# Channel-mix units of 448 tokens that run across batch ends, weights decoded in place of their doubles, shared scratch slots, exponentials in place

## The chip, the cores and the metric

The kernel runs on one core of a Trainium2 chip. The core has five engines with a program each: TensorE (PE, with its weight loads listed apart as PEld), VectorE (DVE), ScalarE (ACT), GpSimd (POOL) and SyncE (SP), which here issues every DMA. They meet at semaphores only. The metric is the device time of one execution in microseconds, lower is better. Three runs of the kernel before took 711.98, 712.05 and 712.50 us, with a median of 712.05.

## The reference

Eight batches of 576 tokens go through windowed attention (8 heads of 64, each query sees its own and the 63 keys before it) and then through a channel mix with two hidden products and a gate:

```python
def _attn_ref(q, k, v):
    scores = scale * np.matmul(q, k.transpose(0, 1, 3, 2))
    mask = (rel >= 0) & (rel < 64)
    scores = np.where(mask, scores, -1e9)
    scores = scores - np.max(scores, axis=-1, keepdims=True)
    attn = np.exp(scores)
    attn = attn / (np.sum(attn, axis=-1, keepdims=True) + 1e-09)
    return np.matmul(attn, v)

def _moe_ref(x, mu_k, mu_r, w_k, w_v, w_r):
    x_prev = ...                       # x one token earlier, zero at a batch's start
    xk = mu_k * x + (1.0 - mu_k) * x_prev
    xr = mu_r * x + (1.0 - mu_r) * x_prev
    k = np.maximum(xk @ w_k, 0.0)      # 512 -> 1024
    v = k * k @ w_v                    # 1024 -> 512
    r = 1.0 / (1.0 + np.exp(-(xr @ w_r)))
    return r * v
```

The weights come as float64, everything else as float32.

## The kernel before

**Attention.** Heads are taken in pairs, which fill the 128 partitions, and a pair's nine blocks of 64 queries in three groups of three. For a group, `scores` makes three score matmuls into PSUM tile `s` (line 149), subtracts mask and finds the minimum on DVE into tile `sm` (152), takes the exponential on ACT into tile `pr` (155), and divides on POOL by the sums (158 to 161). `flip` transposes the three blocks on PE into tile `t` (168) and copies them out (170). `mix_v` takes two groups at once: 12 matmuls of 64 by 64 into tile `x` (182), copied into `xT` (187), which holds a whole batch, channels on partitions; there are two such buffers. Each of these three is a stage; a batch has 42 stages, the later ones of a group behind the next group's first.

**Channel mix.** A unit is half a batch, 288 tokens, so there are 16 units. `time_mix` makes `xr` and `xk` from `xT` chunk by chunk (221 to 226), each split into two float32r parts. The weights are split into two parts too, so each product takes three matmuls per 128 by 128 block of weights: x0 w0, x1 w0, x0 w1 (line 235). Per unit that is 48 matmuls for the gate `r`, 96 for `k` and 96 for `v`: 240, each with 128x128 weights and 288 columns, in 20 steps of 12. ACT, POOL and DVE bring each result out (247 to 253 for the gate, 262 to 266 for the squared hidden values `ks`, 275 for the output), and SP writes it (276). Results go through four PSUM tiles `m`.

**Weights.** 20 chunks of 128 by 512 doubles are loaded into three rotating tiles `wst`, taken apart on DVE by five instructions each (107, 108, 109, 111, 113), and written by ACT and POOL into the tiles `wr_s`, `wk_s`, `wv_s` (116, 117). Twelve chunks are handed out during the first batch's attention, the other eight in the first eight steps of the first unit.

**Order.** The program runs the first batch's attention, mixes the first unit, and then goes through the 320 steps of the units. Each step hands out one attention stage, every sixteenth step two; from step 11 of a unit on, the next unit's mixing goes along. This is only the order in which work is handed to a scheduler, which puts each engine's instructions in an order of its own by dependences, free buffers and an estimated clock. The engines then execute these lists strictly in order.

Of the kernel before, what the change touches and what calls it, by code (L numbers as in the profile page):

```python
# [9 lines left out]
F32 = mybir.dt.float32  # L10
# [32 lines left out]
def attn_rwkv_kernel(ctx, tc, qT, kT, v2, mu_k, mu_r, w_k, w_v, w_r, out):  # L43
# [12 lines left out]
    # queries of a pair by block, the heads' apart: zero where a head's rows meet the  # L56
    # other head's columns
# [24 lines left out]
    # the first group's weights: its first block has none for the other keys  # L82
# [7 lines left out]
    wk_s = const.tile([P, 2, NC, DF], F32R, name="wk_s")  # L90
    wr_s = const.tile([P, 2, NC, DM], F32R, name="wr_s")
    wv_s = const.tile([P, 2, NF, DM], F32R, name="wv_s")

    # A weight comes as a double: its low word and its high word. The float's bits are
    # sign and top exponent bit of the high word, its next 27 bits and 3 bits of the low
    # word; a magnitude outside float32's normal range is brought to its ends first.
    def weights():
        for dst, src in ((wr_s, w_r), (wk_s, w_k), (wv_s, w_v)):
            for c in range(0, dst.shape[3], WC):
                for i in range(dst.shape[2]):  # L100
                    st = tmp.tile([P, WC, 2], U32, name="wst", bufs=WB)
                    nc.sync.dma_start(st.rearrange("p c t -> p (c t)"),
                                      src[i * P:(i + 1) * P, c:c + WC].bitcast(U32))
                    lo, hi = st[:, :, 0], st[:, :, 1]
                    t = tmp.tile([P, WC], U32, name="wt")
                    tf = t.bitcast(F32)
                    nc.vector.tensor_scalar(t, hi, 0x7FFFFFFF, None, op0=ALU.bitwise_and)  # L107
                    nc.vector.tensor_scalar(tf, tf, HI_MIN, HI_MAX, op0=ALU.max, op1=ALU.min)  # L108
                    nc.vector.tensor_scalar(t, t, 3, 0x3FFFFFF8,  # L109
# [5 lines left out]
                    w0, w1 = dst[:, 0, i, c:c + WC], dst[:, 1, i, c:c + WC]  # L115
                    nc.scalar.copy(w0, tf)  # L116
                    nc.gpsimd.tensor_sub(w1, tf, w0.bitcast(F32))  # L117
                    yield

# [1 line left out]
    loaded = {}  # L121
# [245 lines left out]
```

## Time and profile before

| | |
|---|---|
| median of three runs | 712.05 us |
| profiled execution, first to last instruction (span) | 711.3 us |
| around it, to the median | 0.75 us |
| matmul records on PE | 5856, of them 3840 of the channel mix (line 235) |
| busy: PE, DVE, ACT, POOL | 682.2, 415.5, 413.9, 364.9 us |

The page's second part cuts the span into 40 slices of 17.8 us; each digit is the busy share in tenths, 9 being 90% and more. PEclk is the granted TensorE clock, in tenths of full speed.

```profile
PE   6878878999999999999999999999999999999998
DVE  3999999955545455465535455463645556463421
ACT  4768775663626383748566575756756475644351
PEclk9999898999999999999999999999999999999999
```

The first eight slices differ from the rest: there DVE is full and PE is not, afterwards PE is full and no other engine is. The columns of a group row in the views below are: line, engine, operation, output from inputs, shapes, count, then busy us and mean ns of one, then the idle time ahead of them and what ended it. A timeline row has start, length, engine, line, operation and count. Matmuls overlap, so a matmul's own mean time (some 300 ns) is not the distance between two of them; that is read from the starts of rows.

### The profile page before, as it was taken

The page shows a single profiled execution, that of the slowest core. Times are in us where ns is not written, and L with a number is a line of the kernel's source. Part 1 is how long each engine was busy: PE and PEld are TensorE (multiplying, and loading weights), DVE is VectorE, ACT ScalarE, POOL GpSimd, SP SyncE. Part 2 cuts the span into 40 slices and gives each one's busy share as a digit, 9 for nine tenths or more (in the row PEclk, how much of TensorE's full clock was granted, in tenths as well). Part 3 has the DMA queues.
Part 4 walks back from the last instruction along what each step waited for, and adds up shares of the span by engine and source line. Part 5 has one row for each costly group of instructions (what it writes and reads, how often), then busy time and mean ns, then how long its engine had stood idle before and what let it go on. Part 6 is the DMA issues. An engine that isn't in the chain of part 4 may idle for free.

```text
span 711.3 us, 15989 instructions
## 1 busy us (share of the span) xinstructions
PE 682.2 (96%) x5856; PEld 657.9 (92%) x5856; DVE 415.5 (58%) x1326; ACT 413.9 (58%) x1397; POOL 364.9 (51%) x580
## 2 busy tenths in 40 slices
PE   6878878999999999999999999999999999999998
PEld 5766777799999999999999999999999999999998
DVE  3999999955545455465535455463645556463421
ACT  4768775663626383748566575756756475644351
POOL 4788898754335272554626355453624546252420
PEclk9999898999999999999999999999999999999999
DMA  8885666620000001221222222211323221000000
GB/s 208 237 234 152 189 178 176 166 73 26 10 34 2 34 31 64 65 89 45 85 63 72 68 64 88 73 55 44 95 66 94 67 64 48 18 1 35 26 9 34
DMA packets 59742, 56.61 MB, mean 80 GB/s; under 512 B 40592, under 2 KB 49040, under 8 KB 59664
## 3 DMA queue, kind: packets, MB, share of 16 engines
q1 hardware_dynamic: 59664, 55.59, 26.7%
q8 instruction: 46, 0.75, 0.5%
q14 instruction: 32, 0.26, 0.1%
HBM read 46.14 MB, written 9.44 MB: 78 GB/s over the span
## 4 chain that ended last, share of the span: by engine, by line
PE 80%; DVE 15%; POOL 1%; issue 1%; DMA 1%; SPq 1%; ACT 0%
PE m L235 68%; PE s L149 6%; PE x L182 4%; PE t L168 3%; DVE sm L152 2%; DVE wt L111 2%; DVE wt L107 2%; DVE wt L113 2%; DVE xm L224 1%; DVE wt L109 1%; DVE wt L108 1%; DVE rs L158 1%; POOL pr L161 1%; DMA qbd<-qT 1%; DVE d L221 1%
## 5 line engine op out<-in xcount | busy, mean ns | idle before, releaser
L235 PE MATMUL m<-ks,wv_s 128*128 128x288 f32 x1536 | 226.1, 301 | 1.0 <-ACT wv_s L116 0.9
L235 PE MATMUL m<-xk,wk_s 128*128 128x288 f32 x1536 | 221.2, 299 | 2.0 <-POOL wk_s L117 2.0
L161 POOL TENSOR_SCALAR pr<-pr,rs 128x128 f32<-128x128 f32 (+1 forms) x288 | 129.7, 467 | 173.0 <-DVE rs L159 62.4
L235 PEld LDWEIGHTS m<-ks,wv_s 128*128 128x128 f32 x1536 | 208.7, 190 | 2.5 <-ACT wv_s L116 1.3
L235 PEld LDWEIGHTS m<-xk,wk_s 128*128 128x128 f32 x1536 | 207.0, 189 | 3.6 <-POOL wk_s L117 2.2
L155 ACT ACTIVATE pr<-sm,nmax 128x128 f32<-128x128 f32 (+1 forms) x288 | 111.6, 391 | 68.0 <-DVE nmax L152 67.9
L263 POOL TENSOR_TENSOR kf<-kf 128x288 f32<-128x288 f32 x128 | 93.2, 733 | 81.1 <-ACT kf L262 80.1
L266 DVE TENSOR_TENSOR ks<-kf,ks 128x288 fp32r<-128x288 f32 x128 | 72.6, 571 | 71.5 <-ACT ks L265 71.3
L235 PE MATMUL m<-xr,wr_s 128*128 128x288 f32 x768 | 113.1, 299 | 1.0 <-POOL xr L226 1.0
L235 PEld LDWEIGHTS m<-xr,wr_s 128*128 128x128 f32 x768 | 103.5, 188 | 2.4 <-POOL xr L226 1.9
L149 PE MATMUL s<-k,qbd 128*128 128x128 f32 (+1 forms) x576 | 88.4, 294 | 15.7 <-DVE nmax L152 9.0
L149 PEld LDWEIGHTS s<-k,qbd 128*128 128x128 f32 x576 | 79.0, 205 | 19.0 <-DVE nmax L152 11.2
L226 POOL TENSOR_TENSOR xr<-xm,xr 128x288 fp32r<-128x288 f32 x64 | 56.4, 891 | 71.2 <-ACT xr L225 68.4
L152 DVE CUSTOM_DVE_ANT_0 sm<-s,mask 128x128 f32<-128x128 f32 (+1 forms) x288 | 66.7, 276 | 36.1 <-PE s L149 36.0
L262 ACT ACTIVATE kf<-m 128x288 f32<-128x288 f32 x128 | 52.2, 409 | 36.8 <-PE m L235 29.5
L224 DVE SCALAR_TENSOR_TENSOR xm<-d,muk,xT 128x288 f32<-128x288 f32 x64 | 55.2, 862 | 26.7 <-POOL xr L226 26.6
L265 ACT CAST ks<-kf 128x288 fp32r<-128x288 f32 x128 | 55.1, 431 | 24.9 <-POOL kf L263 24.5
L253 DVE SCALAR_TENSOR_TENSOR r<-th,e 128x288 f32<-128x288 f32 x64 | 34.2, 535 | 50.4 <-ACT th L251 50.1
L247 ACT ACTIVATE e<-m 128x288 f32<-128x288 f32 x64 | 26.2, 410 | 60.9 <-PE m L235 60.7
L168 PE MATMUL t<-ident,pr 128*128 128x128 f32 x288 | 55.4, 284 | 6.2 <-POOL pr L161 3.4
L275 DVE SCALAR_TENSOR_TENSOR r<-m,r 128x288 f32<-128x288 f32 x64 | 28.3, 451 | 56.4 <-PE m L235 56.4
L226 POOL TENSOR_TENSOR xk<-xm,xk 128x288 fp32r<-128x288 f32 x64 | 58.5, 933 | 5.2 <-ACT xk L225 5.2
(44 smaller groups left out, 652.7 us busy)
## 6 DMA issues: line engine op xcount, KB each, us to landing
v<-v SPq DMA_DIRECT2D x32, 512.0 KB, 3.6
outT<-r SPq DMA_DIRECT2D x64, 144.0 KB, 1.7
k<-kT SPq DMA_DIRECT2D x31, 288.0 KB, 3.1
qbd<-qT SPq DMA_DIRECT2D x62, 144.0 KB, 3.6
wst<-w_k SPq DMA_DIRECT2D x8, 512.0 KB, 4.1
wst<-w_v SPq DMA_DIRECT2D x8, 512.0 KB, 3.6
wst<-w_r SPq DMA_DIRECT2D x4, 512.0 KB, 7.6
k<-kT SPq DMA_DIRECT2D x1, 192.0 KB, 2.4
```

The source lines that it names most:

```text
L149: nc.tensor.matmul(ps[:, j, :nk], q[:, i].rearrange("p h r -> p (h r)"), k[:, k0:k0 + nk], start=True, stop=True)
L152: nc.vector.tensor_tensor_reduce(sm[:, j, :nk], ps[:, j, :nk], mask if nk == P else mask0, scale=-SCALE, scalar=FAR, op0=ALU.add, op1=ALU.min,
L155: nc.scalar.activation(pr[:, j, :nk], sm[:, j, :nk], AF.Exp, bias=nmax[:, j:j + 1], scale=-1.0, accum_out=sums[:, j:j + 1])
L161: nc.gpsimd.tensor_scalar(pr[:, j, :nk], pr[:, j, :nk], rs[:, j:j + 1], 1.0, op0=ALU.mult, op1=ALU.mult)
L168: nc.tensor.transpose(ps[:, j, :], pr[:, j, :], ident)
L224: nc.vector.scalar_tensor_tensor(xm, d, mu[:, c:c + 1], xp, op0=ALU.mult, op1=ALU.add)
L226: nc.gpsimd.tensor_sub(xs[:, 1, c], xm, xs[:, 0, c].bitcast(F32))
L235: nc.tensor.matmul(ps, w[:, a, c, col * P:(col + 1) * P], x(c, e), start=(i == 0), stop=(i == last))
L262: nc.scalar.activation(kf, ps, AF.Relu)
L263: nc.gpsimd.tensor_mul(kf, kf, kf)
L265: nc.scalar.copy(ks[:, 0], kf)
L266: nc.vector.tensor_sub(ks[:, 1], kf, ks[:, 0].bitcast(F32))
```

## The change

The two first units keep 288 tokens, then come nine of 448: 2 x 288 + 9 x 448 = 4608 = 8 x 576. Six of the nine hold tokens of two batches; for those `time_mix` makes two pieces of each of its DVE instructions, and the output takes two transfers. There are 11 units and 220 steps. Attention stages are handed out so that a unit's last batch is complete when its mixing begins, in equal shares between these points: 34 stages in the first 31 steps, then 42 in each 20 steps, none where a unit needs no new batch (steps 92 to 111), again 42 in each 20 up to step 171.

The decoded weights take, chunk by chunk, slots of the same 20 that the doubles are loaded into (tag `w`). The scratch tiles `d`, `xm`, `e`, `th`, `kf` and `wt`, which had buffers of their own, share six slots (tag `tmp`). The exponential is made in place: `sm` is gone, DVE writes the scores into `pr`, which has three buffers where it had two.

```diff
-TH = S // 2          # tokens of a MoE unit
+UNITS = (288, 288) + (448,) * 9
+TU = max(UNITS)
+USTEPS = 20
+TB = 6
...
-    wk_s = const.tile([P, 2, NC, DF], F32R, name="wk_s")
...
-                    st = tmp.tile([P, WC, 2], U32, name="wst", bufs=WB)
...
-                    t = tmp.tile([P, WC], U32, name="wt")
...
+                st = const.tile([P, WC, 2], U32, name="w", tag="w", bufs=len(chunks))
...
+            tf = tmp.tile([P, WC], F32, name="wt", tag="tmp", bufs=TB)
...
+            ws[i, c] = const.tile([P, 2, WC], F32R, name="ws", tag="w", bufs=len(chunks))
...
-        sm = at.tile([P, G, P], F32, name="sm", bufs=3)
-        pr = pr0 if g == 0 else at.tile([P, G, P], F32, name="pr")
+        pr = pr0 if g == 0 else at.tile([P, G, P], F32, name="pr", bufs=3)
...
-            nc.vector.tensor_tensor_reduce(sm[:, j, :nk], ps[:, j, :nk], mask if nk == P else mask0,
+            nc.vector.tensor_tensor_reduce(pr[:, j, :nk], ps[:, j, :nk], mask if nk == P else mask0,
...
-            nc.scalar.activation(pr[:, j, :nk], sm[:, j, :nk], AF.Exp, bias=nmax[:, j:j + 1], scale=-1.0,
+            nc.scalar.activation(pr[:, j, :nk], pr[:, j, :nk], AF.Exp, bias=nmax[:, j:j + 1], scale=-1.0,
...
+    def parts(u):
+        t, end = sum(UNITS[:u]), sum(UNITS[:u + 1])
+        found = []
+        while t < end:
+            n = min(end, (t // S + 1) * S) - t
+            found.append((t // S, t % S, n))
+            t += n
+        return found
...
+            d = tmp.tile([P, TU], F32, name="d", tag="tmp", bufs=TB)
+            for b, t0, nt in parts(u):
+                xT = xTs[b]
+                x, xp = xT[:, c, 1 + t0:1 + t0 + nt], xT[:, c, t0:t0 + nt]
+                nc.vector.tensor_sub(d[:, o:o + nt], x, xp)
...
+                xm = tmp.tile([P, TU], F32, name="xm", tag="tmp", bufs=TB)
+                for o0, o1, xp in pieces:
+                    nc.vector.scalar_tensor_tensor(xm[:, o0:o1], d[:, o0:o1], mu[:, c:c + 1], xp,
+                                                   op0=ALU.mult, op1=ALU.add)
...
-            run(ats, 1)
-            if done % 16 == 0:
-                run(ats, 1)
...
+    goals = [(0, staged)] + [((u - 1) * USTEPS + MIX_AT, STAGES * (parts(u)[-1][0] + 1))
+                             for u in range(2, len(UNITS))]
+            for (s0, a0), (s1, a1) in zip(goals, goals[1:]):
+                if s0 < done <= s1:
+                    goal = a0 + -(-(a1 - a0) * (done - s0) // (s1 - s0))
+                    run(ats, goal - staged)
+                    staged = goal
```

In the new kernel line 269 is the matmul of line 235, 161 the score matmul, 180 the transpose and 194 the matmul into `x`.

How the scheduler's order moves is shown at three places of PE's list. The first is where the channel mix begins. Before, the first gate product `m` of unit 0 stands behind eight groups of scores `s`:

```order
L149 MATMUL s<-k,qbd_82 128x64
L149 MATMUL s<-k,qbd_82 128x128 x5
L182 MATMUL x<-pt,v 64x64 x6
L168 MATMUL t<-ident,pr 128x128 x3
L182 MATMUL x<-pt,v 64x64 x6
L235 MATMUL m<-xr,wr_s 128x288 x4
L149 MATMUL s<-k,qbd_82 128x128 x3
L235 MATMUL m<-xr,wr_s 128x288 x8
```

Now, at the same product:

```order
L180 MATMUL t<-ident,pr_114 128x128 x2
L194 MATMUL x<-pt,v 64x64 x6
L180 MATMUL t<-ident,pr_114 128x128
L269 MATMUL m<-xr,ws 128x288 x4
L180 MATMUL t<-ident,pr 128x128 x3
L194 MATMUL x<-pt,v 64x64 x3
L269 MATMUL m<-xr,ws 128x288 x8
```

It has moved behind 23 groups: DVE's list has the first mixing of unit 0 behind ten decoded chunks, where it stood behind one. The second place is the end of unit 0, its products into the output (`m<-ks`). Before, they stand among attention, here their first 24 of 96:

```order
L235 MATMUL m<-ks,wv_s 128x288 x4
L149 MATMUL s<-k,qbd_83 128x64
L149 MATMUL s<-k,qbd_83 128x128 x2
L168 MATMUL t<-ident,pr_114 128x128 x3
L235 MATMUL m<-ks,wv_s 128x288 x6
L149 MATMUL s<-k,qbd_83 128x128 x3
L182 MATMUL x<-pt,v 64x64 x6
L235 MATMUL m<-ks,wv_s 128x288 x8
L168 MATMUL t<-ident,pr 128x128 x3
L182 MATMUL x<-pt,v 64x64 x6
L235 MATMUL m<-ks,wv_s 128x288 x6
```

Now they are one run, with nothing of attention among them:

```order
L269 MATMUL m<-xk,ws 128x288 x24
L161 MATMUL s<-k,qbd_83 128x128 x3
L269 MATMUL m<-ks,ws 128x288 x96
L269 MATMUL m<-xr,ws 128x288 x20
L194 MATMUL x<-pt,v 64x64 x3
L269 MATMUL m<-xr,ws 128x288 x28
```

The third place stands for the rest of PE's list, a gate product in the middle. Before, the 12 matmuls into `x` of two groups are one run:

```order
L235 MATMUL m<-xr,wr_s 128x288 x12
L168 MATMUL t<-ident,pr 128x128 x3
L235 MATMUL m<-xr,wr_s 128x288 x12
L182 MATMUL x<-pt,v 64x64 x12
L235 MATMUL m<-xr,wr_s 128x288 x12
L149 MATMUL s<-k,qbd_83 128x128 x3
L235 MATMUL m<-xr,wr_s 128x288 x12
```

Now they are cut in two, with other work between:

```order
L180 MATMUL t<-ident,pr_114 128x128 x3
L269 MATMUL m<-xr,ws 128x448 x5
L194 MATMUL x<-pt,v 64x64 x6
L269 MATMUL m<-xr,ws 128x448 x8
L180 MATMUL t<-ident,pr 128x128 x3
L194 MATMUL x<-pt,v 64x64 x6
L269 MATMUL m<-xr,ws 128x448 x10
L161 MATMUL s<-k,qbd_82 128x128 x3
```

Over all of PE's list, the 48 pairs of groups make 70 runs of `x` before and 103 now. Behind the last mixed stretch of the start (before: the gate products of unit 1; now: the run of 96 above) these lists still hold 51, 58 and 59 groups of `s`, `t` and `x` in 33 runs of `x` before, and 61, 66 and 70 in 77 runs now.

More of the change, by code (lines that the diff above doesn't have):

```diff
@@ L234, in product @@
             for a, e in ((0, 0), (0, 1), (1, 0)):
-                nc.tensor.matmul(ps, w[:, a, c, col * P:(col + 1) * P], x(c, e),
+                nc.tensor.matmul(ps, weight(w, a, c, col), x(c, e),
                                  start=(i == 0), stop=(i == last))
@@ L275, in v_units @@
             nc.vector.scalar_tensor_tensor(o, ps, 0.5, o, op0=ALU.mult, op1=ALU.mult)
-            nc.sync.dma_start(out[b, m * P:(m + 1) * P, half * TH:(half + 1) * TH], o)
+            c0 = 0
+            for b, t0, nt in parts(u):
+                nc.sync.dma_start(out[b, m * P:(m + 1) * P, t0:t0 + nt], o[:, c0:c0 + nt])
+                c0 += nt
             yield
     def new_mixed():
-        return [act.tile([P, 2, NC, TH], F32R, name=nm) for nm in ("xr", "xk")]
+        return [act.tile([P, 2, NC, TU], F32R, name=nm) for nm in ("xr", "xk")]
     def run(g, n=None):
@@ L309, in attn_rwkv_kernel @@
     mixed = new_mixed()
-    run(time_mix(xTs[0], 0, *mixed))
+    run(time_mix(0, *mixed))
     run(ats, LEAD)
+    staged = STAGES + LEAD
+    goals = [(0, staged)] + [((u - 1) * USTEPS + MIX_AT, STAGES * (parts(u)[-1][0] + 1))
+                             for u in range(2, len(UNITS))]
     done = 0
-    for u in range(B * 2):
-        b, half = divmod(u, 2)
+    for u in range(len(UNITS)):
         xr, xk = mixed
@@ L320, in steps @@
         def steps():
-            yield from r_units(xr, gate)
-            yield from k_units(xk, k2)
-            yield from v_units(b, half, k2, gate)
+            yield from r_units(xr, gate, UNITS[u])
+            yield from k_units(xk, k2, UNITS[u])
+            yield from v_units(u, k2, gate)
         for n, _ in enumerate(steps()):
```

100 lines of the change are left out of this document (55 added, 45 removed).

## The prediction

> **What bounds the kernel now.** I read the busy time by stretch first, then the chain of waits. The columns of the stretches are PE, PEld, DVE, ACT and POOL busy with instruction counts, then granted clock, DMA share and GB/s.
>
> ```profile
> 20.00:146.00 126.00, 107.31 (x1001) 92.68 (x1002) 121.52 (x438) 90.75 (x342) 108.23 (x152) 0.93 0.63 184
> 146.00:246.00 100.00, 100.00 (x758) 100.00 (x757) 52.78 (x94) 47.16 (x132) 39.88 (x51) 1.00 0.09 29
> 246.00:628.00 382.00, 382.00 (x3419) 374.43 (x3419) 202.12 (x689) 236.49 (x808) 184.21 (x317) 1.00 0.22 63
> ```
>
> From 146 us on PE is never idle while no other engine passes 62% (ACT, 236.49 of 382). From 20 to 146 us DVE is busy 121.52 of 126 us and PE waits for it. The chain of waits says the same: in the first stretch it runs through DVE lines (decoding 107 to 113, scores 152), in the second through matmuls alone.
>
> ```profile
> by line: DVE sm L152 13.5%; DVE wt L111 12.8%; DVE wt L107 10.3%; DVE wt L113 10.0%; DVE xm L224 8.0%; DVE wt L109 7.5%; DVE wt L108 6.8%; DVE rs L158 4.8%; POOL pr L161 4.4%; issue 4.4%; DVE d L221 4.2%; DVE ks L266 2.9%; DVE rs L159 2.2%;
> ...
> 145.94 98.47 PE m L235 x744
> ```
>
> So there are two questions: when does PE become full, and how much work is left on PE from there. Before, the first answer is 145.9 us and the second 711.3 - 145.9 = 565.4 us.
>
> **The product matmuls.** The 744 of that row take 98.47 us, so a 288-column matmul costs 132.35 ns. What part of it grows with columns? A stretch in which the throttle gave half the clock helps:
>
> ```profile
> 107.80:114.50 6.70, 5.89 (x33) 5.20 (x32) 6.60 (x21) 2.75 (x11) 6.22 (x8) 0.50 0.27 81
> ...
> 112.90 1.64 PE L235 MATMUL m<-ks,wv_s 128*128 128x288 f32 x6
> ...
> 113.62 0.92 PE L235 MATMUL m<-ks,wv_s 128*128 128x288 f32 x3
> ```
>
> Three matmuls later the same run starts 0.72 us later: 240 ns each at half clock, 0.833 ns per column. At full clock the streaming should be half, 120 ns, so 12.35 ns of the 132.35 are something else. For 448 columns the streaming is 448 x 0.4167 = 186.7 ns. That is the lower end. The upper end is that all 132.35 ns grow with columns: 205.9 ns. I take the excess as a cost per matmul, 199.1 ns, between the two; the rows don't settle it.
>
> It isn't the weight load. A load has the same form for scores as for products, and six loads with six matmuls pass in 0.68 us (below), 113 ns each, so the load would be ready before 132 ns are over:
>
> ```profile
> L235 PEld LDWEIGHTS m<-xk,wk_s 128*128 128x128 f32 x1536 | 207.0, 189 | 3.6 <-POOL wk_s L117 2.2
> ...
> L149 PEld LDWEIGHTS s<-k,qbd 128*128 128x128 f32 x576 | 79.0, 205 | 19.0 <-DVE nmax L152 11.2
> ```
>
> The Trainium skill, page "TensorE: Matmul & The Clock Gate", section "Back-to-back issue gap", puts the gap of two matmuls at N/1.2 ns on the slow clock and at N/2.4 + 2.5 ns on the fast one. The first is what the trace has (240 ns), the second would be 122.5 ns and differs from the measured 132.35. By it 448 columns would take 189.2 ns and the 2160 wide matmuls 408.7 us, an estimate from that page.
>
> Behind the point at which PE is full, the old kernel has 3600 product matmuls: 476.5 us. The new one has 336 of 288 columns (44.5 us) and 9 x 240 = 2160 of 448 (430.1 us at 199.1 ns). The term is **-1.9 us**. It is small because 96 products of unit 0 that were done during the start are now behind it (12.7 us); in like for like, 3360 narrow ones at 444.7 us become 430.1.
>
> **The attention left for the full stretch.** Costs on PE from starts of rows, products at 0.1324 us taken out:
>
> ```profile
> 402.14 1.84 PE L235 MATMUL m<-xr,wr_s 128*128 128x288 f32 x12
> 403.82 0.49 PE L168 MATMUL t<-ident,pr 128*128 128x128 f32 x3
> 404.06 1.84 PE L235 MATMUL m<-xr,wr_s 128*128 128x288 f32 x12
> 405.83 0.92 PE L182 MATMUL x<-pt,v 128*64 128x64 f32 x24
> 406.68 1.85 PE L235 MATMUL m<-xr,wr_s 128*128 128x288 f32 x12
> 408.37 0.83 PE L149 MATMUL s<-k,qbd 128*128 128x128 f32 x6
> 408.95 1.84 PE L235 MATMUL m<-xr,wr_s 128*128 128x288 f32 x12
> ```
>
> From 402.14 to 404.06 are 1.92 us, less 12 x 0.1324 = 1.59: a group's transposes cost 0.33 us. In the same way its scores cost 408.95 - 406.68 - 1.59 = 0.68, and two groups' `x` (24 records for 12 matmuls) 406.68 - 404.06 - 1.59 = 1.03. Where `x` was cut:
>
> ```profile
> 348.06 0.54 PE L235 MATMUL m<-ks,wv_s 128*128 128x288 f32 x2
> 348.53 0.57 PE L182 MATMUL x<-pt,v 128*64 128x64 f32 x12
> 349.03 0.40 PE L235 MATMUL m<-ks,wv_s 128*128 128x288 f32 x1
> 349.36 0.45 PE L182 MATMUL x<-pt,v 128*64 128x64 f32 x6
> 349.73 0.66 PE L235 MATMUL m<-ks,wv_s 128*128 128x288 f32 x3
> ```
>
> 12 records cost 0.97 - 0.26 = 0.71 us, 6 cost 0.70 - 0.13 = 0.57. From 12 to 24 records is 0.32 us, 0.027 per record; the rest, **0.38 us, is paid for every run of `x`** however short (0.41 by the 6). So the cutting seen in the order costs: 77 runs behind the start instead of 33, 44 x 0.38 = 16.7 us. Ten more groups of scores are 6.8 us, eight more of transposes 2.6 us, eleven groups of `x` 11 x 12 x 0.027 = 3.6 us. Together **+29.7 us**.
>
> What is left on PE: 565.4 - 1.9 + 29.7 = 593.2 us.
>
> **When PE is full.** Before, the last chunk leaves DVE at 140.27 + 0.74 = 141.0 us:
>
> ```profile
> 140.27 0.74 DVE L113 SCALAR_TENSOR_TENSOR wt<-wst,wt 128x512 uint32<-128x512 uint32 x1
> ```
>
> The decoding is unchanged, 5 x 20 instructions. What else stands ahead of that instruction in DVE's list is less: 33 groups of scores instead of 41 and as many pairs of `rs` instead of 38, 4 `d` instead of 11, 8 `xm` instead of 19, 5 `ks` instead of 8. DVE's groups from 20 to 146 us:
>
> ```profile
> L152 DVE CUSTOM_DVE_ANT_0 sm<-s,mask 128x128 f32<-128x128 f32 (+1 forms) x111 | 25.7, 270 | 0.0
> L111 DVE SCALAR_TENSOR_TENSOR wt<-wst,wt 128x512 uint32<-128x512 uint32 x20 | 19.3, 963 | 0.2
> L113 DVE SCALAR_TENSOR_TENSOR wt<-wst,wt 128x512 uint32<-128x512 uint32 x20 | 17.0, 850 | 0.1
> L107 DVE TENSOR_SCALAR wt<-wst 128x512 uint32<-128x512 uint32 x19 | 14.1, 741 | 2.1 <-POOL wk_s L117 1.5 <-POOL wr_s L117 0.6
> L109 DVE TENSOR_SCALAR wt<-wt 128x512 uint32<-128x512 uint32 x20 | 11.9, 596 | 0.1
> L108 DVE TENSOR_SCALAR wt<-wt 128x512 f32<-128x512 f32 x19 | 10.3, 540 | 0.1
> L158 DVE TENSOR_SCALAR rs<-sums 128x3 f32<-128x3 f32 x35 | 8.9, 254 | 1.8 <-ACT pr L155 1.8
> L152 DVE DVE_READ_ACCUMULATOR2_ANT nmax<- 128x1 f32 x111 | 8.6, 77 | 0.0
> L221 DVE TENSOR_TENSOR d<-xT 128x288 f32<-128x288 f32 x11 | 6.8, 623 | 0.0
> L224 DVE SCALAR_TENSOR_TENSOR xm<-d,mur,xT 128x288 f32<-128x288 f32 x10 | 5.9, 594 | 0.0
> L224 DVE SCALAR_TENSOR_TENSOR xm<-d,muk,xT 128x288 f32<-128x288 f32 x9 | 5.9, 659 | 0.0
> L159 DVE RECIPROCAL rs<-rs 128x3 f32<-128x3 f32 x36 | 5.9, 163 | 0.0
> L266 DVE TENSOR_TENSOR ks<-kf,ks 128x288 fp32r<-128x288 f32 x8 | 4.6, 572 | 0.0
> L253 DVE SCALAR_TENSOR_TENSOR r<-th,e 128x288 f32<-128x288 f32 x4 | 2.3, 590 | 0.0
> L275 DVE SCALAR_TENSOR_TENSOR r<-m,r 128x288 f32<-128x288 f32 x4 | 1.5, 437 | 0.0
> ```
>
> Less are 24 x (0.270 + 0.077) + 5 x (0.254 + 0.163) + 11 x 0.625 + 7 x 0.623 + 3 x 0.572 = 23.4 us by these means. The rows overlap: they add up to 148.7 us in 121.5 us of busy time, a factor of 0.82, so 19.1 us go, and the last chunk is done at 121.9 us. Behind it, ahead of the last `ks` of unit 0, stand 3 `ks`, 2 `d` and 3 `xm`: 4.8 us by the means, 4.0 with the factor. PE can run the first 12 output products (1.6 us) ahead of the last `ks`. PE is full from 121.9 + 4.0 - 1.6 = **124.3 us**. Bounds: 121 us if all of the 23.4 us count (with the 4.8 behind), 134 if the mixing taken out was only filling and the pace is set by attention's chain.
>
> This is earlier by 21.6 us, but 27.8 us of work more are left then: the start covers less of PE's work than it did, because the mixing of unit 0 comes so late that its output products find no place beside DVE.
>
> **What costs nothing.** The wider work of ACT, DVE and POOL lies beside PE. By the busy row of 246 to 628 us ACT fills 62%, and one wide instruction takes the place of 1.56 narrow ones. Attention comes twice as densely in some units and not at all in others, but PE's steps are longer by half too; that in-order queues meet in time is what I rely on, and 1 us of stall is 1 us of time, as PE has no slack. The doubled pieces at batch ends are 12 short DVE instructions in each of six units, and by the same row DVE is free for 47% of the time. The exponential in place removes a buffer, no work; where DVE then waits for a transpose in the start, that is the upper bound above. The shared room and slots remove no instruction.
>
> **Sum.** 124.3 + 593.2 = 717.5 us of span. The median lies 0.75 us above the profiled span; that makes **718.2 us**, 0.9% slower.
>
> **Rivals.** (a) Nothing but streaming grows: the 12.35 ns are hidden by the longer matmul. At 186.7 ns the 2160 cost 26.8 us less: **691 us**, faster. It decides from 196.3 ns per wide matmul downwards, 6.1 us over 2160 below my 199.1. For it: at half clock the excess is nil, so it can vanish. Against: scores pass at 113 ns per load, so the excess is not a load that a longer matmul would cover. Chance 0.15. The formula of the Trainium skill, page "TensorE: Matmul & The Clock Gate", section "Back-to-back issue gap", is of this kind; by its 189.2 ns the time would be 697 us, an estimate from that page. (b) The excess grows with columns: 205.9 ns, +14.7 us, **733 us**. For it: the same vanishing at half clock fits a limit on reading columns. Chance 0.15. (c) The start is shorter: without the mixing among them the attention groups pass faster, and PE is full at 112 us: **706 us**, faster. Against: DVE was idle for only 4.5 of those 126 us, so its list would have to shrink, not its waits. Chance 0.12. (d) The start is longer, as DVE, writing into `pr`, waits for transposes, or dense attention makes stalls: 10 us more, **728 us**. Chance 0.10. My forecast keeps 0.48, with a range of its own of 706 to 728 us: the start's bounds, and below them half the price of the cuts, as only two rows show it.
>
> **How the numbers follow.** A measurement of this kernel can tell some 0.2%, 1.4 us, from no change. Faster: nearly all of (a), most of (c), and a seventh of the forecast, whose range crosses 710.6: 0.32. Within 0.2%: 0.09. Slower: 0.59. The range leaves out (a) and the far half of (b): 700 to 735 us.
>
> **What would show it.** The distance of the wide matmuls in a pure run: 199 ns; 187 is (a), 206 is (b). The start of the run of 96 output products of unit 0: 122 to 125 us; below 115 is (c), above 132 is (d). Runs of `x` of 12 records at some 0.7 us each in the mixed stretches; were they 0.5, 9 us of my sum are gone. PE should still be busy 100% behind the start; idle slices there would be a stall that I haven't counted.

## The result, and the profile after

The changed kernel takes **735.86 us** (median of four runs, 731.59 to 738.68), the kernel before on the same chip 712.01 (711.44 to 712.50). The ratio is **1.033, with an interval of 1.029 to 1.037**: 3.3% slower. The forecast was 718.2 us, 0.9% slower, with a range of 700 to 735; the side is right, the size is not, and the time lies just above the range. The profiled execution has a span of 735.6 us, 18.1 above the 717.5 of the forecast's sum. The explanation goes by this span.

The busy tenths of the page, in slices of 18.4 us:

```profile
PE   6777988699999999899999999999999999999997
DVE  3989788647257337633732923483357336428221
ACT  4667774264754765475344557556745763453530
PEclk9878899899999999999999999999999999999999
```

Of the second to the eighth slice, in which DVE was full (9), only two are full now. PE's digits are lower in three of the first eight slices and higher in two, and the clock row has a 7 and four 8s where it had two 8s. The stretches say it in numbers, in the columns used before:

```profile
20.00:146.00 126.00, 100.12 (x797) 87.04 (x798) 106.23 (x354) 75.55 (x271) 97.23 (x131) 0.86 0.53 155
146.00:246.00 100.00, 99.24 (x716) 91.11 (x714) 52.19 (x149) 55.95 (x162) 45.35 (x62) 1.00 0.19 59
246.00:628.00 382.00, 378.19 (x2557) 337.86 (x2554) 190.09 (x651) 219.68 (x650) 164.54 (x253) 1.00 0.21 61
```

From 20 to 146 us DVE is busy 106.23 us instead of 121.52, so the start has waits that it did not have, and the granted clock is 0.86 instead of 0.93. And behind 146 us PE is no longer full: it misses 0.76 and 3.81 us, where it missed none. The view of PE's waits from 200 to 700 us names what it waits for (us in total, times, longest), 4.2 of 4.5 us in these two rows:

```profile
PE t L180 <- ACT pt L182: 3.2, 2, 1.9
PE x L194 <- ACT pt L182: 1.0, 2, 0.8
```

The distance of the wide matmuls stands in the chain of waits, in a run that nothing else interrupts:

```profile
by line: PE m L269 58.1%; PE s L161 6.1%; PE x L194 5.6%; DVE xm L252 5.6%; PE t L180 3.8%; issue 2.2%; DVE pr L164 2.2%; DVE d L246 2.0%; POOL pr L173 1.5%; DVE wt L122 1.2%; DMA w<-w_k 1.1%; DVE wt L124 1.0%; DVE ks L300 0.9%; DMA w<-w_v 
...
356.36 47.92 PE m L269 x236
...
408.09 2.98 DVE xm L252 x2
...
615.98 115.88 PE m L269 x572
```

115.88 us for 572 matmuls are 202.6 ns each, 47.92 for 236 are 203.1. The first row also has DVE's mixing, `xm` of line 252, with 5.6%. Some of it is behind the start, as the piece of 2.98 us at 408.09, where the forecast had matmuls alone.

The mixed stretches are as forecast. In PE's timeline:

```profile
261.04 0.49 PE L180 MATMUL t<-ident,pr 128*128 128x128 f32 x3
261.28 0.45 PE L269 MATMUL m<-xk,ws 128*128 128x448 f32 x1
261.66 0.57 PE L194 MATMUL x<-pt,v 128*64 128x64 f32 x12
262.16 1.08 PE L269 MATMUL m<-xk,ws 128*128 128x448 f32 x4
263.08 0.83 PE L161 MATMUL s<-k,qbd 128*128 128x128 f32 x6
263.66 1.87 PE L269 MATMUL m<-xk,ws 128*128 128x448 f32 x8
265.37 0.49 PE L180 MATMUL t<-ident,pr 128*128 128x128 f32 x3
```

From 261.04 to 263.08 are 2.04 us, less five products at 0.203: 1.03 us for a group's transposes (0.33) and a run of `x` of 12 records, which leaves 0.70 for that run; forecast was 0.7. From 263.08 to 265.37, less eight products, the scores take 0.67.

What the forecast did not have is the end of unit 0, the run of 96 output products that was to take 12.7 us:

```profile
117.12 8.04 PE L269 MATMUL m<-ks,ws 128*128 128x288 f32 x47 [1.96 <-ACT kf L296]
125.57 5.25 PE L269 MATMUL m<-ks,ws 128*128 128x288 f32 x33 [0.41 <-ACT ks L299]
132.51 0.80 PE L269 MATMUL m<-ks,ws 128*128 128x288 f32 x4 [1.69 <-ACT ks L299]
134.03 1.87 PE L269 MATMUL m<-ks,ws 128*128 128x288 f32 x12 [0.72 <-DVE ks L300]
139.64 5.17 PE L269 MATMUL m<-xr,ws 128*128 128x288 f32 x20 [3.74 <-DVE r L310]
```

It begins at 117.12, before the 124.3 of the forecast, after a wait for ACT's read of a finished `k` product, and stops three times for the hidden values `ks`. The next products wait 3.74 us more for line 310, DVE's read of the finished output out of PSUM. DVE's own timeline shows why that is late:

```profile
124.57 1.04 DVE L124 SCALAR_TENSOR_TENSOR wt<-w,wt 128x512 uint32<-128x512 uint32 x1
...
127.83 1.53 DVE L246 TENSOR_TENSOR d<-xT 128x288 f32<-128x288 f32 x1
...
133.53 0.45 DVE L300 TENSOR_TENSOR ks<-kf,ks 128x288 fp32r<-128x288 f32 x1
...
138.18 1.04 DVE L252 SCALAR_TENSOR_TENSOR xm<-d,muk,xT 128x288 f32<-128x288 f32 x1
139.14 1.55 DVE L310 SCALAR_TENSOR_TENSOR r<-m,r 128x288 f32<-128x288 f32 x4
```

In DVE's list the four reads stand behind the whole mixing of unit 1, four `d` and eight `xm` with the last `ks` among them, which takes from 127.83 to 139.14: 11.3 us, where the means that the forecast used (0.62 each, 0.57 for `ks`) make 8.0. The first and the third row are the end of the last chunk's decoding, at 125.6 us, and the last `ks` of unit 0, done at 134.0.

**Where the 18.1 us are.** The cut is unit 1's first `k` product. By the forecast it starts at 124.3 + 12.7 + 48 x 0.1324 + some 0.4 for the `x` between = 143.7 us and leaves 573.8. Measured are 149.9 and 585.7. So the start has 6.2 us of the miss and what lies behind it 11.9. In the start the run of 96 begins 7.2 us early and takes 9.8 us longer (22.5 instead of 12.7, the wait at its end included), and the gate products behind it take 10.3 us instead of 6.8. From 139.6 to 144.8 us the granted clock is 0.50, and the first 20 gate products take 5.17 us, 258 ns each. Of the 11.9 us, (202.6 - 199.1) ns x 2160 are 7.6. Six places at which two matmuls are 0.5 to 2.3 us apart (6.7 us, of which the usual distance makes some 1.3) are about 5.4. The remainder is -1.1: 75 runs of `x` and 68.7 groups of `x` were left, where the order had shown 77 and 70.

### The profile page after: what moved, and what is told of

Read it like the earlier page. It is cut to its first block, busy times and chain, and to the rows that moved or that the text cites. A ratio compares the mean times of both kernels' runs of the same rounds, so it can differ in the third digit from the quotient of the medians.

```text
span 735.6 us, 13202 instructions
## 1 busy us (share of the span) xinstructions
PE 694.1 (94%) x4656; PEld 622.5 (85%) x4656; DVE 393.4 (53%) x1258; ACT 400.2 (54%) x1197; POOL 345.6 (47%) x500
## 4 chain that ended last, share of the span: by engine, by line
PE 74%; DVE 17%; POOL 3%; DMA 2%; issue 2%; ACT 2%; SPq 0%; POOLq 0%; ACTq 0%; DVEq 0%
PE m L269 58%; PE s L161 6%; PE x L194 6%; DVE xm L252 6%; PE t L180 4%; DVE pr L164 2%; DVE d L246 2%; POOL pr L173 2%; DVE wt L122 1%; DMA w<-w_k 1%; DVE wt L124 1%; DVE ks L300 1%; DMA w<-w_v 1%; DVE wt L118 1%; DVE wt L120 1%
## 5 line engine op out<-in xcount | busy, mean ns | idle before, releaser
L269 PE MATMUL m<-ks,ws 128*128 128x448 f32 (+1 forms) x1056 | 215.2, 358 | 4.9 <-ACT ks L299 2.1
L269 PE MATMUL m<-xk,ws 128*128 128x448 f32 (+1 forms) x1056 | 219.1, 358 | 0.7 <-ACT kf L296 0.5
L269 PEld LDWEIGHTS m<-ks,ws 128*128 128x128 f32 x1056 | 186.9, 190 | 18.6 <-ACT ks L299 2.6
L269 PEld LDWEIGHTS m<-xk,ws 128*128 128x128 f32 x1056 | 183.6, 188 | 14.4 <-ACT kf L296 0.7
L297 POOL TENSOR_TENSOR kf<-kf 128x448 f32<-128x448 f32 (+1 forms) x88 | 82.3, 936 | 168.1 <-ACT kf L296 165.6
L167 ACT ACTIVATE pr<-pr,nmax 128x128 f32<-128x128 f32 (+1 forms) x288 | 111.2, 390 | 35.2 <-DVE nmax L164 34.8
L269 PE MATMUL m<-xr,ws 128*128 128x448 f32 (+1 forms) x528 | 114.3, 367 | 3.7 <-DVE r L310 3.7
L269 PEld LDWEIGHTS m<-xr,ws 128*128 128x128 f32 x528 | 95.1, 196 | 10.8 <-DVE r L310 4.0
L164 DVE CUSTOM_DVE_ANT_0 pr<-s,mask 128x128 f32<-128x128 f32 (+1 forms) x288 | 65.8, 276 | 66.0 <-PE s L161 57.5
L194 PE MATMUL x<-pt,v 128*64 128x64 f32 x1152 | 59.3, 236 | 2.3 <-ACT pt L182 1.6
```

The costliest lines, as they stand in the source:

```text
L164: nc.vector.tensor_tensor_reduce(pr[:, j, :nk], ps[:, j, :nk], mask if nk == P else mask0, scale=-SCALE, scalar=FAR, op0=ALU.add, op1=ALU.min,
L167: nc.scalar.activation(pr[:, j, :nk], pr[:, j, :nk], AF.Exp, bias=nmax[:, j:j + 1], scale=-1.0, accum_out=sums[:, j:j + 1])
L194: nc.tensor.matmul(ps[h * W:(h + 1) * W, e, j, :], v[:, a, c, h * W:(h + 1) * W], pt[:, j, h * W:(h + 1) * W], start=True, stop=True)
L269: nc.tensor.matmul(ps, weight(w, a, c, col), x(c, e), start=(i == 0), stop=(i == last))
L297: nc.gpsimd.tensor_mul(kf, kf, kf)
```

## The experiments

### Is the distance of the wide matmuls a cost per matmul, or does it grow?

e1 is 144 matmuls each of seven widths one behind the other, with the same form of weights and data, and nothing else on PE:

```diff
+    order = (128, 192, 256, 288, 352, 448, 512)
+        for i in range(144):
+            nc.tensor.matmul(ps, w[:, (i % 4) * P:(i % 4 + 1) * P], x[:, i % 3, :n],
+                             start=(i == 0), stop=(i == 143))
```

> Only matmuls: 144 each of 128, 192, 256, 288, 352, 448 and 512 columns with float32r operands and 128x128 weights, nothing of the reference's result is computed. Read is the distance between starts. Theory (part of the excess grows with columns, as 132.4 ns at 288 and 202.6 ns at 448 in the changed kernel ask): about 0.439 ns per column plus 6 ns, so 174 at 352, 203 at 448, 231 at 512. Rival 1 (a cost per matmul, the step of the prediction): 159 at 352, 199 at 448, 226 at 512. Rival 2 (203 is made by what goes on beside the matmuls in the kernel): 199 or less at 448 here, where nothing else runs.

Measured at the full clock, from starts: 111.7 ns for 192 columns, 120.0 for 256, 131.7 for 288, 160.0 for 352, 202.7 for 448, 226.7 for 512. (The 128 columns ran at half the clock and give no figure.) From 256 to 512 each column adds (226.7 - 120.0) / 256 = 0.4168 ns, as the forecast had it. 448 has 202.7 here too, so the distance belongs to the matmul and not to what stands around it in the kernel. The excess over 0.4167 ns per column is 13.3 ns at 256, 352 and 512 columns, 11.7 at 288 and 16.0 at 448. So e5 did the same with the widths around:

```diff
-    order = (128, 192, 256, 288, 352, 448, 512)
+    order = (384, 400, 416, 432, 448, 480, 512)
```

> Only matmuls again, 144 each of 384, 400, 416, 432, 448, 480 and 512 columns; nothing of the reference's result is computed. The operand's rows are 448 columns apart up to 448 (as in the changed kernel) and 512 apart beyond. In the first run of this kind the excess over 0.4167 ns per column was 13.3 ns at 256, 352 and 512, 11.7 at 288 and 16.0 at 448. Theory (about 13.3 ns per matmul, and 448 happens to be a dear width): 173.3 at 384, 180 at 400, 186.7 at 416, 193.3 at 432, 202 to 203 at 448, 213.3 at 480. Rival (the excess grows with columns): 432 at 195 or more, 480 at 216 or more.

PE's timeline of e5, one row for a stretch inside each width:

```profile
14.75 15.41 PE L70 MATMUL m<-y,w 128*128 128x384 f32 x88
...
64.73 20.50 PE L70 MATMUL m<-y,w 128*128 128x416 f32 x108
...
91.80 18.38 PE L70 MATMUL m<-y,w 128*128 128x432 f32 x93
...
119.74 20.43 PE L70 MATMUL m<-y,w 128*128 128x448 f32 x100
...
149.83 20.53 PE L70 MATMUL m<-x,w 128*128 128x480 f32 x94
...
181.72 18.52 PE L70 MATMUL m<-x,w 128*128 128x512 f32 x81
```

A row's length holds the last matmul's own time of some 0.36 to 0.39 us: (20.43 - 0.365) / 99 = 202.7 ns for 448, (18.52 - 0.389) / 80 = 226.6 for 512, 173.3 for 384, 188.3 for 416, 195.9 for 432, 216.7 for 480, and 180.0 from the starts at 400. The excess over streaming is 13.3 ns at 384, 400 and 512, and 15.0, 15.8, 16.0 and 16.7 at 416, 432, 448 and 480. Neither expectation of e5 holds over all widths. The forecast's picture, a cost per matmul, holds from 256 to 400 and at 512 (13.3 ns, and 11.7 at 288, where the forecast had 12.35). 448 is one of four widths here that cost 1.7 to 3.4 ns more; why is open.

### What does each part do by itself?

Four kernels: the one before with the shared slots alone (e2), with the exponential in place alone (e11), with the weights in the room of their doubles alone (e12), and the change with the old units (e3), so with all three. The edits of e2 and e3, cut:

```diff
-            d = tmp.tile([P, TH], F32, name="d")
+            d = tmp.tile([P, TH], F32, name="d", tag="tmp", bufs=6)
...
-UNITS = (288, 288) + (448,) * 9
+UNITS = (288,) * 16
...
+            run(ats, 1)
+            if done % 16 == 0:
+                run(ats, 1)
```

> The kernel before with one part of the change: d, xm, e, th, kf and wt share six slots. Theory (the shared slots delay unit 0's mixing, so that PE has less to do while DVE decodes): PE's list then has unit 0's first product behind 27 groups of scores instead of 8; slower by 4 to 12 us, 716 to 724. Rival (the slots cost nothing, the start is late for other reasons): 712.

> The changed kernel with 16 units of 288 tokens and the old hand-out of attention; shared slots, weights in the room of their doubles and the exponential in place stay. Theory (two thirds of the loss come with the wide units: x cut in two, three late mixings; the rest from the start): 716 to 724 us, 132.4 ns per matmul, PE without idle time behind the start. Rival (the loss is that of the start and of the shared room): 730 or more.

> The kernel before with the exponential in place alone (no sm, three pr); nothing is left out. Theory (e3 less e2 leaves 1 to 2 us for the exponential and the weights' room together): 710.5 to 714 us. Rival (DVE waits for transposes in the start): 716 us or more.

> The kernel before with the weights decoded into the slots of their doubles alone; nothing is left out. Theory: 710.5 to 714 us. Rival (a decoded chunk waits until its slot's doubles are read, and this holds the decoding up): 716 us or more. Rival (three loads ahead where slots are 20 lets loads run freer): 708 us or less.

Measured: e2 722.61 us, 1.016 (1.014 to 1.018); e3 724.72, 1.019 (1.017 to 1.021); e11 712.99, 1.002 (1.001 to 1.003); e12 713.51, 1.002 (1.001 to 1.003). Those are the times of their first theories, e3 0.7 us above its upper end. Against the kernel before on the same chip (710.90 and 711.53 us) the slots alone cost 11.7 us of the 23.9, the exponential and the room 1.5 and 2.0, and the three together 13.8. The other 10 come with the units of 448 and the hand-out of attention that goes with them. That is less than the two thirds that e3's theory gave them. In e2's stretch from 20 to 146 us

```profile
20.00:146.00 126.00, 101.75 (x846) 89.84 (x845) 112.56 (x374) 80.23 (x285) 95.11 (x130) 0.91 0.58 161
```

DVE is busy 112.56 us instead of 121.52, as in the change (106.23): its first product starts at 70.7 us, where it starts at 23.8 before, and 58, 66 and 70 groups of `s`, `t` and `x` are left behind unit 1's first `k` product instead of 51, 58 and 59. That is the forecast's second term, seen alone.

### What does a cut of `x` cost?

e4 is the kernel before with each group's `x` handed out by itself:

```diff
-            if t >= 2 and len(a2) >= 2 and t % 2:
-                mix_v(a2[:2], xT)
-                del a2[:2]
+            if a2 and t >= 2:
+                mix_v(a2[:1], xT)
+                del a2[:1]
```

> The kernel before with one cost doubled: the matmuls into x are made group by group, so that PE's list has 65 runs of x instead of 34 behind unit 0's products. Theory (0.38 us for every run of x): 31 more runs, +11 us, 723. Rival (a run of x costs what its matmuls cost): 712.

725.05 us, 1.020 (1.018 to 1.022). Behind unit 1's first `k` product 64 runs are left instead of 33, and 570.5 us instead of 559.2. One more group of scores (0.67) taken off, 10.6 us for 31 runs are **0.34 us per run**; the forecast had 0.38 from two rows.

### Is it the late first mixing, or the late hand-out?

e6 is e2 with unit 0's mixing handed out during the first batch's attention. e7 is the change with attention handed out eight steps earlier. e8 is e7 with the mixing early, and a step between a group's transposes and its `x`:

```diff
+        if i in (17, 23, 35, 41):
+            run(mix0, 2)
...
-    goals = [(0, staged)] + [((u - 1) * USTEPS + MIX_AT, STAGES * (parts(u)[-1][0] + 1))
+    goals = [(0, staged)] + [((u - 1) * USTEPS + MIX_AT - 8, STAGES * (parts(u)[-1][0] + 1))
```

> The kernel before with the shared slots (as e2, 722.6) and unit 0's mixing handed out chunk by chunk during the first batch's attention, ahead of the later chunks of weights. Theory (what the shared slots cost is that unit 0's mixing gets its slots late): PE's list has the first product behind 14 groups instead of 27, and the time comes back by at least half, 711 to 717. Rival (the cost of the shared slots lies elsewhere, in the decoding or in the later units): within 2 us of e2.

> The changed kernel with attention handed out eight steps earlier, so that a batch is complete well before the unit that crosses into it is mixed. PE's list then has 59 runs of x instead of 77 behind unit 0. Theory (0.38 us for every run of x, and about 5 us of PE waiting for late mixings): 735.9 - 7 - 5 = 724 (721 to 728). Rival 1 (only the waits): 731. Rival 2 (neither): 736.

> As e7, with unit 0's mixing handed out during the first batch's attention as in e6, and the matmuls into x never in the same step as the transpose ahead of them (61 runs of x behind unit 0). Theory (the late start is worth some 10 us of the loss): 712 to 719. Rival (the start costs nothing beyond e7): within 2 us of e7.

e6: 719.01 us, 1.009 (1.008 to 1.011); the first product starts at 34.4 instead of 70.7 us, and that is worth 3.6 us against e2 (4.7 when each is set against the kernel before on its own chip). The time is above the 711 to 717 of its theory. e7: 728.64, 1.023 (1.021 to 1.025), just above the 721 to 728 of its theory. It has 57 runs of `x` instead of 75, and 18 x 0.34 = 6 us of the 7 won would be these. The waits behind the start, which its theory had as won too, have moved and not gone: PE is idle there for 6.1 us instead of 4.5, and in the view of PE's waits from 200 us on it has

```profile
PE x L194 <- ACT xT L199: 5.5, 4, 1.6
```

e8: 731.09, 1.025 (1.021 to 1.029), where 712 to 719 were expected, so its theory falls. Unit 1's first `k` product is at 136.9 instead of 148.6 us, but 592.5 us are left instead of 580.2. Of these 12.3 us some 4 are five more groups of scores and two of transposes that stand behind that point now, and 2.5 are idle time of PE (8.6 us instead of 6.1); the rest was not taken apart. The late first mixing is not, by itself, what makes the change slow.

### Do the units need to be 448 wide?

e9 has twelve units of 384 (the width with the small excess), which leave room for scratch buffers of their own; e10 is the same with the shared slots. Both also put a step between a group's transposes and its `x`, as e8 does, and hand attention out by a rule that counts unit 1:

```diff
-UNITS = (288, 288) + (448,) * 9
+UNITS = (384,) * 12
...
-            d = tmp.tile([P, TU], F32, name="d", tag="tmp", bufs=TB)
+            d = tmp.tile([P, TU], F32, name="d", bufs=2)
```

> The change with twelve units of 384 instead of 2 x 288 and 9 x 448, with scratch buffers of their own (d 2, xm 3, e, th, kf, wt 2 each) instead of the six shared slots, with a group's transposes and the matmuls into x handed out in different steps, and with attention for unit 1 counted in the hand-out; nothing is left out of the computation. Theory (the shared slots make the long start, 448 is a dear width, and the pieces at batch ends make the stalls behind the start): products 2880 x 173.3 ns = 499.2 us instead of 508.2 before, 86 runs of x instead of 70 (+5.5 us), start as before (idle 49 us), and 6 to 7 us of stalls behind it: 710 to 717 us. Rival (the stalls behind the start come from the shared slots): 703 to 709 us. Rival (dense attention itself makes the start and the stalls long, slots or not): 720 to 730 us.

> The same as the units of 384 with buffers of their own, but with the change's six shared slots; nothing is left out. Theory (the slots cost what they cost alone, 10 to 12 us): 9 to 13 us above the kernel with buffers of its own. Rival (with wide units the slots cost nothing of their own): within 3 us of it.

e9: 715.77 us, 1.006 (1.004 to 1.007); e10: 719.54, 1.011 (1.010 to 1.013). In both PE is never idle behind 151 us, though four of the twelve units hold tokens of two batches, and e10 has the slots. So neither slots nor batch ends make the waits behind the start by themselves. The slots cost 3.8 us here, less than alone, and neither of e10's expectations (9 to 13 us, or within 3) holds. e9's first theory holds in time (710 to 717) but not in its reason, the 6 to 7 us of waits. As PE is never idle behind the start, what the theory's sum lacks must be in the start, and that wasn't followed further.

### What holds DVE?

What was left open is what makes PE wait behind the start. The timeline of the change at its longest wait there:

```profile
295.92 0.15 DVE L170 TENSOR_SCALAR rs<-sums 128x3 f32<-128x3 f32 x1
...
300.34 1.16 POOL L255 TENSOR_TENSOR xr<-xm,xr 128x448 fp32r<-128x448 f32 x1 [0.90 <-ACT xr L254]
...
300.54 0.98 DVE L170 TENSOR_SCALAR rs<-sums 128x3 f32<-128x3 f32 x1
...
301.44 0.61 DVE L310 SCALAR_TENSOR_TENSOR r<-m,r 128x448 f32<-128x448 f32 x1
...
302.05 0.19 DVE L164 CUSTOM_DVE_ANT_0 pr<-s,mask 128x64 f32<-128x64 f32 x1
...
302.34 0.35 ACT L167 ACTIVATE pr<-pr,nmax 128x64 f32<-128x64 f32 x1 [1.61 <-DVE nmax L164]
...
302.69 0.46 ACT L182 COPY pt<-t 128x384 f32<-128x384 f32 x1
...
303.29 0.41 PE L180 MATMUL t<-ident,pr 128*128 128x128 f32 x2 [1.92 <-ACT pt L182]
```

Read from below: PE's transposes wait 1.92 us for the copy `pt`, which frees their one PSUM buffer. The copy stands on ACT behind an exponential that waits 1.61 us for DVE's scores. DVE's scores stand behind two reads of the output and a `rs` of three columns that takes **0.98 us**. The same instruction takes 0.15 us in the first row. It began while POOL's subtraction `xr` (300.34 to 301.50) ran and ended with it. Counted over all records behind 160 us: `rs` takes 0.17 us where POOL does nothing, and 0.63 on the mean and up to 1.11 beside a two-input instruction of POOL; `xm` of 448 columns takes 0.67 us where POOL does nothing and 1.31 on the mean beside one, `d` of 448 columns 0.61 and 0.96. The reciprocal, the scores out of PSUM and the output's read out of PSUM are no longer beside POOL than without. So some of DVE's instructions on SBUF are held until POOL is through. In the 7 us ahead of each of the four places at which PE is idle, the held `xm`, `d` and `rs` together take 2 to 3 us more than the quickest of their form do; PE's idle time there is 0.5 to 1.9 us.

The Trainium skill, page "SBUF — State Buffer", section "Who interferes with whom", says that VectorE and GpSimd share a pair of ports under an exclusive lock, which whoever issues first has for the whole instruction. By that section a VectorE instruction with two inputs in SBUF contends with a GpSimd instruction that reads SBUF, a tensor-scalar one can, and one with a single input outside the modes that use both ports doesn't. The rows of `xm` and `d` (two inputs) and of `rs` (tensor-scalar) agree, and so does the reciprocal, with one input, which isn't held (0.16 us beside POOL, 0.17 without). In which mode `rs` ran, no trace here shows.

In the units of 448 POOL's subtraction is 1.32 us long and eight of them fall into each mixing. The test is to take it off POOL: in the change (e13), in the kernel before (e14), in the units of 384 (e15) and in e8 (e16).

```diff
-                nc.gpsimd.tensor_sub(xs[:, 1, c, :n], xm[:, :n], xs[:, 0, c, :n].bitcast(F32))
+                nc.vector.tensor_sub(xs[:, 1, c, :n], xm[:, :n], xs[:, 0, c, :n].bitcast(F32))
```

> The change with the mixing's subtraction (line 255, xm less its rounded part) on DVE instead of POOL; nothing is left out. Theory (DVE's xm and d are held while POOL's two-input subtraction runs, and this makes the stalls behind the start): xm of 448 takes some 0.5 us on the mean instead of 0.9, the 6.7 us of stalls behind the start fall below 2, and 726 to 731 us. Rival (dense attention as such makes them): the stalls stay, 734 to 742 us, as DVE has 0.6 us x 8 more per unit.

> The kernel before with the mixing's subtraction (line 226) on DVE instead of POOL; nothing is left out. Theory (behind the start PE is never idle, so only the start can change; there 16 subtractions of 0.46 us, 7.3 us, come to DVE and the waits of xm and d beside POOL go, about 0.4 us each of some 20): 708 to 714 us. Rival (DVE bounds the start and every instruction counts): 716 to 720 us.

> The units of 384 with buffers of their own (e9) with the mixing's subtraction on DVE; nothing is left out. Theory (the start's second mixing is held beside POOL): 707 to 713 us. Rival (DVE bounds the start): 717 us or more.

> The change with attention handed out 8 steps earlier, transposes and x apart and the first mixing earlier (e8), and the mixing's subtraction on DVE; nothing is left out. Theory (POOL beside xm makes the waits for xT behind the start): 7 to 9 us below e8's 731.1, 721 to 725 us. Rival (dense attention makes them): 729 us or more.

e13: **719.38 us, 1.012 (1.010 to 1.014): 16.5 us less** than the change, more than its theory said, by an edit that gives DVE eight instructions more per unit. e14: 711.38, 1.000 (0.999 to 1.001): in the kernel before it does nothing. e16: 720.53, 1.015 (1.010 to 1.020), 10.6 below e8, with two of its four runs near 717.5 us and two near 723.5. e15: 715.17, 1.006 (1.004 to 1.008), as e9 without it; its theory falls, and what e9 loses in the start isn't this. The mixing's rows of the change, from 160 to 640 us:

```profile
L252 DVE SCALAR_TENSOR_TENSOR xm<-d,mur,xT 128x448 f32<-128x448 f32 x8 | 8.7, 1088 | 0.1
...
L252 DVE SCALAR_TENSOR_TENSOR xm<-d,muk,xT 128x448 f32<-128x448 f32 x8 | 8.1, 1009 | 0.0
```

and of e13, with its stretches:

```profile
L252 DVE SCALAR_TENSOR_TENSOR xm<-d,muk,xT 128x448 f32<-128x448 f32 x6 | 4.2, 692 | 0.0
L252 DVE SCALAR_TENSOR_TENSOR xm<-d,mur,xT 128x448 f32<-128x448 f32 x6 | 4.2, 692 | 0.0
```

```profile
20.00:146.00 126.00, 104.92 (x881) 92.06 (x882) 110.79 (x377) 83.18 (x295) 90.86 (x118) 0.93 0.54 159
146.00:246.00 100.00, 100.00 (x720) 91.32 (x719) 52.91 (x184) 58.69 (x171) 26.26 (x49) 1.00 0.22 63
246.00:628.00 382.00, 382.00 (x2555) 343.59 (x2554) 184.81 (x683) 217.28 (x636) 111.42 (x201) 1.00 0.21 62
```

The wide `xm` takes 0.69 us instead of 1.05, PE is full again behind 146 us, and from 246 to 628 us DVE is busy for 184.81 us, where the change has 190.09, though the mixing gives it more to do. Of the 18.6 us by which the span is shorter, 10.7 are in the start (unit 1's first `k` product at 139.2 instead of 149.9) and 7.9 behind it. The waits behind the start go with POOL's subtraction in both pairs: PE's idle time there falls from 4.5 us in the change and from 8.6 in e8 to nothing in e13 and e16. The scheduler's lists change there too, on PE and ACT as well as on DVE, so a part of the new order in this isn't excluded; the hold itself stands in the rows of the change. The subtraction is not enough alone: e9 and e10 have it on POOL and have no such waits. In the start the edit also rearranges the lists (three of the four reads of line 310 stand ahead of the mixing's last two subtractions), and the clock is 0.93 instead of 0.86; how much of the 10.7 us is each was not taken apart.

### The rest of POOL's two-input work

The square of the hidden values is such an instruction too. e17 is e13, and e18 the kernel before with e14's edit, each with that square on ACT:

```diff
-            nc.gpsimd.tensor_mul(kf, kf, kf)
+            nc.scalar.activation(kf, kf, AF.Square)
```

> The change with the mixing's subtraction on DVE and the square of kf (line 297) as an activation on ACT instead of a product on POOL; nothing is left out. Theory (POOL's square holds DVE's subtraction into ks in the start too, up to 0.6 us in each of 16): 713 to 718 us, below e13's 719.4. Rival (what is left of the start is the slots' doing, and ACT's 16 squares of some 0.4 us more in the start make up for it): 719 to 723 us.

> The kernel before with the mixing's subtraction on DVE and the square on ACT; nothing is left out. Theory (POOL's square holds DVE in the start): 705 to 709.5 us, faster than before. Rival (as e14, no change in the start): 710.5 to 714 us.

e17: 718.02 us, 1.009 (1.008 to 1.011), against e13's 1.012 (1.010 to 1.014): the intervals overlap, so for the change it settles nothing. e18: **706.15 us, 0.993 (0.991 to 0.994)**, the best of all the kernels here, 0.7% faster than the one before. In its stretch

```profile
20.00:146.00 126.00, 109.46 (x1050) 94.73 (x1051) 119.14 (x475) 97.40 (x365) 89.35 (x136) 0.97 0.68 190
```

PE does 1050 records instead of 1001, with DVE nearly as full as before (119.14 instead of 121.52 us), POOL less busy (89.35 instead of 108.23) and the clock at 0.97 instead of 0.93. How much of the gain is the hold that its theory names, and how much the new order and the clock, was not taken apart.

## Why the prediction was right on the side and wrong on the size

**The product matmuls: a term mis-sized.** "I take the excess as a cost per matmul, 199.1 ns" was right as a picture (e1: 13.3 ns at 256 and at 512) and 3.5 ns short for 448, a width that costs more than its neighbours 384 and 512 (e5). Over 2160 that is 7.6 us. Rival (a) (187) is out. At 448 alone the 203 of the pure run lies as near to the 206 of rival (b) as to 199; what puts (b) out is 512, where it would have 235 ns and 226.7 were measured.

**The attention left behind the start: right.** 61, 66 and 69 groups in 75 runs are left, nearly as the order had shown, a run of `x` of 12 records takes 0.70 us, and e4 has 0.34 us per cut, which would make the 16.7 us of cuts some 15. e2 shows the other half of the term alone.

**When PE is full: wrong.** "PE is full from 121.9 + 4.0 - 1.6 = 124.3 us" assumed that DVE's list shrinks and keeps its pace. It did shrink, but the last chunk left DVE at 125.6 us instead of 121.9, and from there to the last `ks` it took 8.4 us instead of 4.0. The run of 96 began at 117 and took 22.5 us instead of 12.7, and the gate products behind it ran at half the clock at first. The estimate also looked at what stands ahead of the last chunk and of the last `ks`, and not at what stands ahead of the reads that free PSUM: the rest of unit 1's mixing, which took 11.3 us in all where the means promised 8.0. The marker given for it, the start of the run of 96, was ill chosen: it came early while the run stopped and went. Net the start is 6.2 us late. That is what rival (d) said, with 10 us; its reason, DVE waiting for transposes as it writes into `pr`, exists (5.2 us of DVE's waits up to 146 us are put down to `t`), but alone the exponential in place costs 1.5 us (e11).

**What costs nothing: wrong, and the main step that failed.** "The wider work of ACT, DVE and POOL lies beside PE", because no engine was over 62% busy, and "that in-order queues meet in time is what I rely on". They did not: PE was idle for 4.5 us behind the start, which cost some 5.4, the sign that the prediction had named for such a stall. A share of busy time doesn't show that two engines which are both half free exclude each other. With the mixing's subtraction taken off POOL (e13) these waits go, a longer part of the start goes with them, and the change takes 719.4 us, near the 718.2 that the forecast gave without this effect. The nearness is partly luck, since the wide distance is still 3.5 ns over it. By its 16.5 us it is the largest step, but by the spans more than half of that lies in the start, where order and clock change too.

The sign was there to be read in the rows that the prediction quotes: `rs`, 128x3, has a mean of 254 ns, and half of these 35 take 156 ns or less. A mean that far above the usual time of one form was, here, an instruction that is being held.

## What to carry to other kernels

Before a change makes instructions longer on an engine that "has room", compare the mean with the shortest of the same form: a gap can say that something holds them, as here, and a longer neighbour may then hold them longer. When work is moved or merged, list what stands on the in-order engine ahead of the read that frees the matmul's output buffer, and not only ahead of its inputs. And measure a matmul's distance at the width that is to be used: here 384, 400 and 512 columns have the smaller excess and 416 to 480 do not.

## What the runs showed of the hardware that was not expected

- The distance of 128x128 matmuls of this type is 0.4167 ns per column and 13.3 ns at 256, 352, 384, 400 and 512 columns, 11.7 at 288, but 15.0 to 16.7 ns at 416, 432, 448 and 480 (e1, e5).
- DVE's `rs`, `d` and `xm` are held while POOL runs a two-input instruction (`rs` 0.17 against up to 1.11 us; at 448 columns `xm` 0.67 against 1.31 and `d` 0.61 against 0.96 on the mean); its reciprocal and what it reads from PSUM are not.
- The granted clock from 20 to 146 us lay between 0.86 and 0.97 in these kernels and did not simply follow PE's busy time: it is 0.97 in e4 with PE busy for 103.57 us, 0.93 before with 107.31, and 0.86 in the change with 100.12 and in e15 with 109.21.
